# Layer one of a Fourier mix and two expert layers: ScalarE's relus ahead of its side work, stage A behind four result products

## Chip, cores and metric

The kernel runs on one core of one Trainium2 chip. Its five engines work through queues of their own, in order: TensorE (PE, with the weight loads as PEld), VectorE (DVE), ScalarE (ACT), GpSimd (POOL) and SyncE (SP, which issues most DMAs). The metric is the device time of one execution in microseconds. In the tables a result of TensorE lies in PSUM, in banks of 512 columns of float32; everything else lies in SBUF.

## What is computed

```python
X = fft(fft(x, axis=1), axis=2).real          # x: 2 x 3008 x 256
h = X @ w_in                                  # 6016 tokens, 256 -> 2048
g = maximum(h, 0) + alpha * minimum(h, 0)
x2 = g @ w_out                                # 2048 -> 256
h2 = x2 @ w_in2
out = (h2 * sigmoid(h2)) @ w_out2             # 256 -> 2048 -> 256
```

All matrices are float32, and products are made from parts: a value is split in a high part and the rest ("hi" and "lo"), and three products (hi hi, lo hi, hi lo) stand for one.

## The kernel before

The sequence transform is done as a transform of 47 by 64 points. For batch 0 it is done at the start (stage U, then psB). For batch 1 a stage A (`back_stage_a`) runs beside layer one: a piece of x is loaded (`xr`), split into `xhl` by ScalarE (line 367) and GpSimd (line 371), multiplied by a constant (`stage_a`, lines 377 to 379, tile psA), copied out by ScalarE as `ev` (line 406) and written to DRAM (`tmid`). There are 16 such pieces. Stage B (`stage_b`, psB, line 422) makes the tokens' features `pq` from it, again as hi (line 437) and lo (line 441). `rank_one` (psR, line 482, copied out as `rsb` in line 485) makes a row that is added to the even products. The tiles psA, psB, psR and psW share one PSUM bank (tag "x").

Layer one is a loop over 6 chunks `c` of 512 tokens (450 in the first) and 16 blocks `m` of 128 hidden units, 96 steps. In a step TensorE makes the even and the odd half of h in one bank (`products1`, line 602, three matmuls each). `column1` (line 622, VectorE) reads the bank after the even products, as `h`. Line 645 (VectorE) gets the mirrored token's value from the bank and `h`, into the bank psd ("h2"). Lines 646 and 647 (ScalarE) are the relus of both, into `r`, and line 651 (VectorE, twice) finishes the activation in `r`; it reads the bank too, so the bank is free only after its first half. There are two banks "h", two tiles `r`, three `gh` and two `gl`.

`close1`, called at the start of the next step, copies `r` to `gh` (ScalarE, line 666) and takes the rest to `gl` (GpSimd, line 667). The result products (`second1`, line 682, 12 matmuls a step: eight with `gh`, then four with `gl`) are kept in a queue, and `pull(n)` issues n of them. With `LAG1` = 1, a step pulls the products of two steps earlier.

`step1` also issues the even products of the next step ahead (`ahead`), if they are ready. All other work is written as generators that stop at phases: `advance(AMID)` and the like run them on by one stop. EARLY lies at the start of a step, before `close1`. At BANK the lo copies of psB and psW (lines 441, 576) are issued. At AMID come stage A's products with `ev`, psR with `rsb`, and the conversions of weights from 64 bit (`narrow`: lines 227 and 228 on ScalarE), and differences of the halves. At MID1 and MID2 come the later parts of the conversions (lines 233, 235) and, in the first step of all, a column sum (psS, line 559) and the mix of weight block 2 (`early_mix`, psW, line 553).

So the queue of each engine follows the order in which `step1` calls these. Before, it is: odd products, even products of the next step, eight result products, BANK, AMID, four result products, psd, relus, `column1` of the next step, line 651, then MID1 to MID3.

Of the kernel before, what the change touches and what calls it, by code (L numbers as in the profile page):

```python
# [25 lines left out]
NF = DFF // P  # L26
KG = 4
CK = 8
NC = B * H1 // CK
# [13 lines left out]
def _width(c):  # L43

    return AT0 + OWN if c == 0 else CK * N2
# [52 lines left out]
def kernel(  # L98
# [54 lines left out]
    def ptile(shape, name, tag="x"):  # L153
        return psh.tile(shape, F32, name=name, tag=tag, bufs=2 if tag == "h" else 1)

    def wtile(shape, dtype, name, tag):
        return work.tile(shape, dtype, name=name, tag=tag, bufs=BUFS[tag])
# [10 lines left out]
    EARLY, AMID, LATE, BANK, MID1, MID2, MID3 = range(1, 8)  # L168
    active = []

    def advance(phase):
        for job in list(active):
            if job[1] == phase:
                job[1] = next(job[0], 0)
                if not job[1]:
                    active.remove(job)
# [420 lines left out]
    def products1(c, m, eo, bank):  # L597

        w = _width(c)
        q, mm = divmod(m, 4)  # L600
        for a, bb in ((0, 0), (1, 0), (0, 1)):
            T.matmul(bank[:, :w], wa[q][:, mm, eo, a, :], pq[c][:, 2 * eo + bb, :w], start=eo == 0 and a == bb,  # L602
                     stop=bb == 1, skip_group_check=True)

    def ready1(c, m):

        if c == 0:
            return m // 2 in mixed and m // 2 in sums
        return c in rows and (c != HOST or guests) and sum(k == c for k, _ in turned) == CK // KG

    def even(c, m):

        assert ready1(c, m)
        bank = ptile([P, 512], "psh", "h")
        products1(c, m, 0, bank)
        return bank

    def column1(c, m, bank):

        w = _width(c)  # L620
        t = wtile([P, 512], F32, "h", "h")
        V.scalar_tensor_tensor(t[:, :w], pb[c][:, :w], wst[:, m:m + 1], bank[:, :w], op0=ALU.mult, op1=ALU.add)  # L622
        evens[c, m] = bank, t

    def step1(c, m):

        w = _width(c)
        n = 12 if len(queue) > LAG1 else 0
        if (c, m) not in evens:
            column1(c, m, even(c, m))  # L630
            pull(min(n, 8))
            n -= min(n, 8)
        bank, t = evens.pop((c, m))
        assert c in rows
        products1(c, m, 1, bank)
        c1, m1 = divmod(c * NF + m + 1, NF)
        ahead = even(c1, m1) if c1 < NC and ready1(c1, m1) else None
        pull(min(n, 8))
        n -= min(n, 8)
        advance(BANK)  # L640
        advance(AMID)
        pull(n)
        r = wtile([P, 2, 512], F32, "r", "r")
        other = ptile([P, 512], "psd", "h2")
        V.scalar_tensor_tensor(other[:, :w], t[:, :w], 2.0, bank[:, :w], op0=ALU.mult, op1=ALU.subtract)  # L645
        A.activation(r[:, 0, :w], bank[:, :w], AF.Relu, scale=-1.0)  # L646
        A.activation(r[:, 1, :w], other[:, :w], AF.Relu, scale=-1.0)
        if ahead is not None:
            column1(c1, m1, ahead)
        for s, h in enumerate((bank, other)):  # L650
            V.scalar_tensor_tensor(r[:, s, :w], r[:, s, :w], al[:, m:m + 1], h[:, :w], op0=ALU.mult, op1=ALU.add)  # L651
        save_due()
        advance(MID1)
        advance(MID2)
        advance(MID3)
        return c, m, r
# [34 lines left out]
    def save_due():  # L691
        while due:
            save_x2(due.pop())
# [20 lines left out]
    def pull(n):  # L714

        while n and queue:
            if next(queue[0], 0) is None:
                n -= 1
            else:
                queue.pop(0)  # L720
# [232 lines left out]
    with tc.manual_schedule():  # L953
# [30 lines left out]
        for i in range(nx):  # L984
# [5 lines left out]
            if i in BEHIND:  # L990
                kind, n = BEHIND[i]
# [59 lines left out]
        for eo, h in ((0, 0), (0, 1), (1, 0), (1, 1)):  # L1051
            n = CK // 2
# [61 lines left out]
        for c in range(NC):  # L1114
            for m in range(NF):
                early(c * NF + m)
                close1(last)
                last = step1(c, m)
                advance(LATE)
# [93 lines left out]
```

## Time and profile before

| | us |
|---|---|
| median of 3 runs | 966.06 (964.96 to 966.13) |
| the profiled execution | 965.77 |
| its span, first to last instruction | 964.0 |
| TensorE matmuls busy | 946.1 (98%) |
| TensorE weight loads busy | 792.3 (82%) |
| VectorE / ScalarE / GpSimd busy | 630.2 / 588.3 / 529.6 |

The profile is of one execution. A matmul is shown from its start to a modelled end, so that matmuls in sequence overlap. "Idle before" of a row is the time that its engine stood before it, with the instruction that released it. Layer one's steps lie between some 29 and 476 us.

### The profile page before, as it was taken

What the parts mean: (1) busy time and instruction counts of PE and PEld (TensorE: products, weight loads), DVE (VectorE), ACT (ScalarE), POOL (GpSimd) and SP (SyncE); (2) the same over time, 40 slices, a digit from 0 to 9 for tenths busy, and PEclk for the clock granted to TensorE, in tenths of its full rate; (3) what the DMA queues carried; (4) which work ended last, traced back from release to release, by engine and by line L of the source; (5) the groups of instructions that cost most, each with busy time, mean ns of one, the idle gap of its engine ahead of it and who ended that gap; (6) DMA issues with size and microseconds to landing.
All of it is one profiled execution on the core that took longest, in us unless ns stands there. A gap on an engine that the chain in (4) does not pass through costs nothing.

```text
span 964.0 us, 12344 instructions
## 1 busy us (share of the span) xinstructions
PE 946.1 (98%) x4351; PEld 792.3 (82%) x4351; DVE 630.2 (65%) x953; ACT 588.3 (61%) x996; POOL 529.6 (55%) x347
## 2 busy tenths in 40 slices
PE   9899999998999999999999999999999999999998
PEld 9799876776888878888899988888888888888886
DVE  4667654675777678777576765676576566657554
ACT  5787655565666557656666664665575565556654
POOL 0488767564456458998985733543354254334322
PEclk9999999999999999999999999999999999999999
DMA  9411112213422320021010020010010001001001
GB/s 330 151 44 50 33 50 69 71 48 111 161 66 99 110 66 23 1 66 33 12 44 23 1 83 1 1 44 1 1 44 1 1 1 44 1 1 45 0 1 45
DMA packets 30394, 47.60 MB, mean 49 GB/s; under 512 B 4118, under 2 KB 11388, under 8 KB 30076
## 3 DMA queue, kind: packets, MB, share of 16 engines
q1 hardware_dynamic: 29756, 45.98, 14.9%
q8 instruction: 34, 0.56, 0.2%
q10 hardware_dynamic: 576, 0.84, 0.2%
q14 instruction: 28, 0.23, 0.1%
HBM read 33.28 MB, written 13.52 MB: 49 GB/s over the span
## 4 chain that ended last, share of the span: by engine, by line
PE 94%; ACT 2%; DVE 2%; issue 1%; POOL 0%; ACTq 0%; POOLq 0%; DVEq 0%
PE pso L878 27%; PE pso L682 24%; PE psh L808 23%; PE psh L602 13%; PE psB L422 2%; PE psU L1015 2%; DVE r L651 1%; PE psW L553 1%; ACT r L646 1%; PE psA L379 0%; ACT raw L228 0%; PE psA L377 0%; PE psA L378 0%; PE idle L966 0%; PE psB L1055 0%
## 5 line engine op out<-in xcount | busy, mean ns | idle before, releaser
L829 DVE TENSOR_TENSOR ring<-ring,psh 128x512 f32<-128x512 f32 (+1 forms) x336 | 222.3, 674 | 168.3 <-PE psh L808 156.1
L878 PE MATMUL pso<-ghl,wAo 128*128 128x512 f32 (+1 forms) x1152 | 309.8, 385 | 0.0
L667 POOL TENSOR_TENSOR gl<-r,gh 128x1024 fp32r<-128x1024 f32 (+1 forms) x96 | 226.6, 2361 | 103.2 <-ACT gh L666 84.5
L808 PE MATMUL psh<-ts,wi 128*128 128x512 f32 (+1 forms) x1008 | 278.9, 385 | 0.0
L820 POOL TENSOR_TENSOR ghl<-ring,ghl 128x512 fp32r<-128x512 f32 (+1 forms) x96 | 137.6, 1433 | 255.5 <-ACT ghl L815 175.7
L878 PEld LDWEIGHTS pso<-ghl,wAo 128*128 128x128 f32 x1152 | 216.3, 188 | 40.6
L832 ACT ACTIVATE ring<-ring 128x512 f32<-128x512 f32 (+1 forms) x192 | 119.7, 623 | 178.0 <-DVE ring L829 176.1
L808 PEld LDWEIGHTS psh<-ts,wi 128*128 128x128 f32 x1008 | 189.3, 188 | 35.3
L682 PE MATMUL pso<-gh,wo_o 128*128 128x512 f32 (+1 forms) x768 | 187.8, 386 | 0.0
L682 PEld LDWEIGHTS pso<-gh,wo_o 128*128 128x128 f32 x768 | 144.3, 188 | 27.6
L602 PE MATMUL psh<-pq,wa 128*128 128x512 f32 (+1 forms) x576 | 153.7, 395 | 12.6 <-DVE r L651 10.2
L602 PEld LDWEIGHTS psh<-pq,wa 128*128 128x128 f32 x576 | 105.1, 188 | 41.7 <-DVE r L651 19.7
L666 ACT ACTIVATE gh<-r 128x1024 fp32r<-128x1024 f32 (+1 forms) x96 | 100.2, 1043 | 63.1 <-DVE r L651 60.3
L651 DVE SCALAR_TENSOR_TENSOR r<-r,al,psh 128x512 f32<-128x512 f32 (+1 forms) x96 | 70.8, 737 | 80.4 <-ACT r L646 77.2
L815 ACT ACTIVATE ghl<-ring 128x512 fp32r<-128x512 f32 (+1 forms) x192 | 119.2, 621 | 6.1
L682 PE MATMUL pso<-gl,wo_o 128*128 128x512 f32 (+1 forms) x384 | 102.2, 387 | 0.0
L645 DVE SCALAR_TENSOR_TENSOR psd<-h,psh 128x512 f32<-128x512 f32 (+1 forms) x96 | 65.5, 682 | 43.1 <-PE psh L602 41.0
L682 PEld LDWEIGHTS pso<-gl,wo_o 128*128 128x128 f32 x384 | 71.8, 188 | 13.9
L820 DVE TENSOR_TENSOR ghl<-ring,ghl 128x512 fp32r<-128x512 f32 (+1 forms) x96 | 76.6, 798 | 5.5 <-ACT ghl L815 5.3
L646 ACT ACTIVATE r<-psh 128x512 f32<-128x512 f32 (+1 forms) x96 | 55.8, 581 | 31.9 <-DVE psd L645 30.0
L622 DVE SCALAR_TENSOR_TENSOR h<-pb,wst,psh 128x512 f32<-128x512 f32 (+1 forms) x96 | 70.4, 734 | 1.6 <-PE psh L602 1.5
L651 DVE SCALAR_TENSOR_TENSOR r<-r,al,psd 128x512 f32<-128x512 f32 (+1 forms) x96 | 70.2, 732 | 0.0
(97 smaller groups left out, 647.3 us busy)
## 6 DMA issues: line engine op xcount, KB each, us to landing
raw<-in_w_in SPq DMA_DIRECT2D x16, 512.0 KB, 5.7
raw<-in_w_out SPq DMA_DIRECT2D x16, 512.0 KB, 5.0
out_dram<-ob SPq DMA_DIRECT2D x19, 256.0 KB, 2.3
x<-in_x SPq DMA_DIRECT2D x6, 512.0 KB, 6.0
xr<-in_x SPq DMA_DIRECT2D x16, 192.0 KB, 2.6
tmid<-ev SPq DMA_DIRECT2D x48, 64.0 KB, 1.7
ur<-tmid SPq DMA_DIRECT2D x6, 512.0 KB, 7.2
stash_o<-y SPq DMA_DIRECT2D x8, 256.0 KB, 3.2
```

The costliest lines, as they stand in the source:

```text
L602: T.matmul(bank[:, :w], wa[q][:, mm, eo, a, :], pq[c][:, 2 * eo + bb, :w], start=eo == 0 and a == bb, stop=bb == 1, skip_group_check=True)
L622: V.scalar_tensor_tensor(t[:, :w], pb[c][:, :w], wst[:, m:m + 1], bank[:, :w], op0=ALU.mult, op1=ALU.add)
L651: V.scalar_tensor_tensor(r[:, s, :w], r[:, s, :w], al[:, m:m + 1], h[:, :w], op0=ALU.mult, op1=ALU.add)
L666: A.activation(hi[:, :, :w], r[:, :, :w], AF.Copy)
L667: G.tensor_tensor(lo[:, :, :w], r[:, :, :w], f32(hi[:, :, :w]), op=ALU.subtract)
L682: T.matmul(po[c][s][k][:, :w], wo1[q][:, mm, a, k * P:(k + 1) * P], g[:, s, :w], start=m == 0 and a == 0 and g is hi, stop=m == NF - 1 and ...
L808: T.matmul(bank[j][:, :w], wi2[p][:, FORMS[j], a], t[:, :w], start=a == 0 and t is hi, stop=t is lo)
L815: A.activation(outs[p, i][:, 0, :w], g[:, :w], AF.Copy)
L820: eng.tensor_tensor(hl[:, 1, :w], g[:, :w], f32(hl[:, 0, :w]), op=ALU.subtract)
L829: V.tensor_tensor(dst[:, :w], a[:, :w], bank[j][:, :w], op=ALU.add)
L832: A.activation(a[:, :w], a[:, :w], AF.Silu)
L878: T.matmul(po[c, 2][s][k][:, :w], wo2[q][:, mm + m, a, k * P:(k + 1) * P], outs[p, i][:, g, :w], start=p == 0 and i < 2 and a == 0 and g == 0,
```

## The change

In `step1` the relus (and line 645) are now issued before `advance(BANK)` and `advance(AMID)`, so the side work of a step comes behind them on ScalarE, and the lo copies behind line 645 on VectorE. `column1` of the next step comes behind BANK but ahead of the result products. These are pulled as four, then AMID, then eight, where it was eight, BANK, AMID, four. Where a step's even products are not issued yet (the first step of a chunk whose inputs were not ready), and nothing can be pulled (the very first step), the even products of the next step and `advance(MID1)` come ahead of the odd products.

```diff
--- before.py
+++ after.py
@@ -626,27 +626,32 @@
 
         w = _width(c)
         n = 12 if len(queue) > LAG1 else 0
+        following = divmod(c * NF + m + 1, NF)
+        ahead = None
         if (c, m) not in evens:
             column1(c, m, even(c, m))
-            pull(min(n, 8))
-            n -= min(n, 8)
+            if n:
+                pull(8)
+                n -= 8
+            else:
+                ahead = even(*following)
+                advance(MID1)
         bank, t = evens.pop((c, m))
         assert c in rows
         products1(c, m, 1, bank)
-        c1, m1 = divmod(c * NF + m + 1, NF)
-        ahead = even(c1, m1) if c1 < NC and ready1(c1, m1) else None
-        pull(min(n, 8))
-        n -= min(n, 8)
-        advance(BANK)
-        advance(AMID)
-        pull(n)
+        if ahead is None and following[0] < NC and ready1(*following):
+            ahead = even(*following)
         r = wtile([P, 2, 512], F32, "r", "r")
         other = ptile([P, 512], "psd", "h2")
         V.scalar_tensor_tensor(other[:, :w], t[:, :w], 2.0, bank[:, :w], op0=ALU.mult, op1=ALU.subtract)
         A.activation(r[:, 0, :w], bank[:, :w], AF.Relu, scale=-1.0)
         A.activation(r[:, 1, :w], other[:, :w], AF.Relu, scale=-1.0)
+        advance(BANK)
         if ahead is not None:
-            column1(c1, m1, ahead)
+            column1(*following, ahead)
+        pull(min(n, 4))
+        advance(AMID)
+        pull(n - min(n, 4))
         for s, h in enumerate((bank, other)):
             V.scalar_tensor_tensor(r[:, s, :w], r[:, s, :w], al[:, m:m + 1], h[:, :w], op0=ALU.mult, op1=ALU.add)
         save_due()
```

Lines behind the change are numbered five higher in the changed kernel: 645, 646, 647, 651, 666, 667 and 682 become 646, 647, 648, 656, 671, 672 and 687.

ScalarE in a stage A step with a conversion, before (`gh` of the step before, then `ev`, the conversion, the relus):

```order
L666 ACTIVATE gh<-r 128x1024
L406 ACTIVATE ev<-psA 96x512
L227 ACTIVATE y_1856<-raw_1817 128x512
L228 ACTIVATE raw_1817<-raw_1817 128x512
L646 ACTIVATE r<-psh 128x512
L647 ACTIVATE r<-psd 128x512
L666 ACTIVATE gh<-r 128x1024
```

and in the changed kernel:

```order
L671 ACTIVATE gh<-r 128x1024
L647 ACTIVATE r<-psh 128x512
L648 ACTIVATE r<-psd 128x512
L406 ACTIVATE ev<-psA 96x512
L227 ACTIVATE y_1856<-raw_1817 128x512
L228 ACTIVATE raw_1817<-raw_1817 128x512
L671 ACTIVATE gh<-r 128x1024
```

`ev` and the two conversions moved behind the two relus.

TensorE around a stage A product, before (psh are the even and odd products, pso the result products):

```order
L602 MATMUL psh<-pq_927,wa_232 128x512 x6
L682 MATMUL pso<-gh,wo_o_355 128x512 x8
L377 MATMUL psA<-xhl,cat 96x512
L378 MATMUL psA<-xhl,cat 96x512
L379 MATMUL psA<-xhl,cat 96x512
L682 MATMUL pso<-gl,wo_o_355 128x512 x4
L602 MATMUL psh<-pq_927,wa_232 128x512 x3
L602 MATMUL psh<-pq_927,wa_388 128x512 x3
```

and in the changed kernel:

```order
L602 MATMUL psh<-pq_927,wa_232 128x512 x6
L687 MATMUL pso<-gh,wo_o_355 128x512 x4
L377 MATMUL psA<-xhl,cat 96x512
L378 MATMUL psA<-xhl,cat 96x512
L379 MATMUL psA<-xhl,cat 96x512
L687 MATMUL pso<-gh,wo_o_355 128x512 x4
L687 MATMUL pso<-gl,wo_o_355 128x512 x4
L602 MATMUL psh<-pq_927,wa_232 128x512 x3
L602 MATMUL psh<-pq_927,wa_374 128x512 x3
```

The three psA matmuls moved from behind the eighth to behind the fourth result product.

TensorE at the start of layer one, before (the last psB of the start, then psh: even 0, odd 0, even 1):

```order
L1055 MATMUL psB<-cbt,u_all 128x64 x8
L602 MATMUL psh<-pq_117,wa_232 128x450 x9
L559 MATMUL psS<-ones,wq 128x2 x2
L553 MATMUL psW<-wq,cwt 128x256 x4
L602 MATMUL psh<-pq_117,wa_232 128x450 x6
L422 MATMUL psB<-cbt,u_all 128x64 x8
L602 MATMUL psh<-pq_117,wa_232 128x450 x6
```

and in the changed kernel:

```order
L1060 MATMUL psB<-cbt,u_all 128x64 x8
L602 MATMUL psh<-pq_117,wa_232 128x450 x6
L559 MATMUL psS<-ones,wq 128x2 x2
L553 MATMUL psW<-wq,cwt 128x256 x4
L602 MATMUL psh<-pq_117,wa_232 128x450 x9
L422 MATMUL psB<-cbt,u_all 128x64 x8
L602 MATMUL psh<-pq_117,wa_232 128x450 x6
```

Odd 0 moved behind psS and psW: ahead of these now stand even 0 and even 1, behind them odd 0, odd 1 and even 2.

VectorE in the same first steps, before (h is `column1`):

```order
L622 SCALAR_TENSOR_TENSOR h<-pb,wst,psh 128x450
L645 SCALAR_TENSOR_TENSOR psd<-h,psh 128x450
L622 SCALAR_TENSOR_TENSOR h<-pb,wst,psh 128x450
L651 SCALAR_TENSOR_TENSOR r<-r,al,psh 128x450
L651 SCALAR_TENSOR_TENSOR r<-r,al,psd 128x450
L233 TENSOR_SCALAR y_359<-y_359 128x512
L576 TENSOR_TENSOR wa_388<-psW,wa_388 128x2x2x128
L645 SCALAR_TENSOR_TENSOR psd<-h,psh 128x450
```

and in the changed kernel:

```order
L622 SCALAR_TENSOR_TENSOR h<-pb,wst,psh 128x450
L646 SCALAR_TENSOR_TENSOR psd<-h,psh 128x450
L576 TENSOR_TENSOR wa_374<-psW,wa_374 128x2x2x128
L622 SCALAR_TENSOR_TENSOR h<-pb,wst,psh 128x450
L656 SCALAR_TENSOR_TENSOR r<-r,al,psh 128x450
L656 SCALAR_TENSOR_TENSOR r<-r,al,psd 128x450
L233 TENSOR_SCALAR y_359<-y_359 128x512
L646 SCALAR_TENSOR_TENSOR psd<-h,psh 128x450
```

The lo copy of psW (line 576) moved ahead of the second `column1`.

## Rows read from the trace of the kernel before

**Rows 1.** The page, parts 1 and 5: totals, and three groups of layer one

```profile
PE 946.1 (98%) x4351; PEld 792.3 (82%) x4351; DVE 630.2 (65%) x953; ACT 588.3 (61%) x996; POOL 529.6 (55%) x347
...
L667 POOL TENSOR_TENSOR gl<-r,gh 128x1024 fp32r<-128x1024 f32 (+1 forms) x96 | 226.6, 2361 | 103.2 <-ACT gh L666 84.5
...
L651 DVE SCALAR_TENSOR_TENSOR r<-r,al,psh 128x512 f32<-128x512 f32 (+1 forms) x96 | 70.8, 737 | 80.4 <-ACT r L646 77.2
...
L645 DVE SCALAR_TENSOR_TENSOR psd<-h,psh 128x512 f32<-128x512 f32 (+1 forms) x96 | 65.5, 682 | 43.1 <-PE psh L602 41.0
```

**Rows 2.** Busy us of each engine by stretch, then clock, DMA share, GB/s

```profile
30.00:42.00 12.00, 9.27 (x45) 7.89 (x44) 7.60 (x13) 7.08 (x17) 4.90 (x4) 0.86 0.21 70
33.80:37.00 3.20, 3.20 (x11) 2.71 (x10) 2.49 (x5) 1.05 (x3) 0.32 (x1) 0.50 0.00 0
42.00:105.00 63.00, 62.92 (x320) 57.49 (x320) 44.29 (x73) 47.49 (x87) 53.67 (x34) 1.00 0.14 44
105.00:244.00 139.00, 129.78 (x563) 101.11 (x561) 81.55 (x119) 80.22 (x129) 86.18 (x44) 1.00 0.27 73
360.00:480.00 120.00, 120.00 (x532) 99.59 (x531) 87.45 (x124) 78.84 (x119) 109.02 (x76) 1.00 0.10 30
```

**Rows 3.** Waits of TensorE's matmuls: us, times, longest

```profile
PE psh L602 <- DVE r L651: 10.2, 17, 1.5
```

**Rows 4.** Waits of TensorE's weight loads: us, times, longest

```profile
PEld psh L602 <- DVE r L651: 19.7, 25, 1.9
```

**Rows 5.** Timeline, TensorE, two plain steps: start, us, engine, line, tile

```profile
292.13 1.98 PE L682 MATMUL pso<-gh,wo_o 128*128 128x512 f32 x8
...
296.21 1.98 PE L682 MATMUL pso<-gh,wo_o 128*128 128x512 f32 x8
```

**Rows 6.** Timeline of a step with stage A

```profile
155.73 0.40 PE L377 MATMUL psA<-xhl,cat 96*96 96x512 f32 x1
...
156.43 1.09 PE L682 MATMUL pso<-gl,wo_o 128*128 128x512 f32 x4
156.67 0.60 ACT L406 ACTIVATE ev<-psA 96x512 f32<-96x512 f32 x1 [1.86 <-PE psA L379]
...
157.17 0.59 ACT L646 ACTIVATE r<-psh 128x512 f32<-128x512 f32 x1
...
157.35 0.84 PE L602 MATMUL psh<-pq,wa 128*128 128x512 f32 x3
...
158.59 0.98 PE L602 MATMUL psh<-pq,wa 128*128 128x512 f32 x3 [0.40 <-DVE r L651]
...
161.26 0.39 PE L377 MATMUL psA<-xhl,cat 96*96 96x512 f32 x1
```

**Rows 7.** Stage A's first products, all: durations, first and last start

```profile
L377 PE MATMUL psA<-xhl,cat x16: 392/396/397, 105.0 to 231.9; 96*96 96x512 f32 x16
```

**Rows 8.** Timeline of a stage A step with a conversion

```profile
202.46 0.65 ACT L227 ACTIVATE y<-raw 128x512 f32<-128x512 f32 x1
...
202.69 0.84 PE L602 MATMUL psh<-pq,wa 128*128 128x512 f32 x3
...
204.97 0.97 PE L602 MATMUL psh<-pq,wa 128*128 128x512 f32 x3 [1.44 <-DVE r L651]
```

**Rows 9.** Timeline, a conversion without stage A

```profile
352.02 0.98 PE L602 MATMUL psh<-pq,wa 128*128 128x512 f32 x3 [0.99 <-DVE r L651]
```

**Rows 10.** Timeline of layer one's first two steps

```profile
31.76 0.66 DVE L622 SCALAR_TENSOR_TENSOR h<-pb,wst,psh 128x450 f32<-128x450 f32 x1
...
32.57 1.65 PE L602 MATMUL psh<-pq,wa 128*128 128x450 f32 x6 [2.27 <-DVE h L622]
...
34.73 3.12 PE L553 MATMUL psW<-wq,cwt 128*128 128x256 f32 x8
...
37.50 1.58 PE L602 MATMUL psh<-pq,wa 128*128 128x450 f32 x6
...
42.65 0.57 PE L682 MATMUL pso<-gh,wo_o 128*128 128x450 f32 x2
```

## Prediction

> **What bounds the kernel now.** I read the totals by engine first, then the busy time by stretch, then who waits for whom, and the order of time last. The totals show a kernel bound by TensorE: 946.1 of 964.0 us, the other engines at two thirds or less [rows 1]. So a gain can only come from time in which TensorE does not issue. The stretches say where that is [rows 2]: 30 to 42 us (9.27 of 12 busy, with the granted clock at its lower level, 0.50, for 3.2 us) and 105 to 244 us (129.78 of 139). From 42 to 105 and from 360 to 480 next to nothing is lost. The waits name the cause: 17 times TensorE stood before line 602 until VectorE's line 651 had run, 10.2 us in all [rows 3]. The same wait seen from the weight loads is 19.7 us in 25 times [rows 4]. The first figure is too small, since a matmul is drawn until its result is out, long after the next could have been issued; the second is too large, since a weight load normally runs ahead. The loss lies between.
>
> The order of time shows the chain. `even` of step m+2 needs the bank of step m, which line 651 releases, and that follows the relu of line 646 on ScalarE. In a step with a stage A product [rows 6], `ev` (line 406) stands ahead of the relu, and ScalarE waits 1.86 us for psA, the last side work of TensorE there. Only then come the relu (157.17) and line 651, and TensorE, which began its odd products at 157.35, is held before the next even ones until 158.59. psA to psA takes 161.26 - 155.73 = 5.53 us in this step. A step without side work takes 296.21 - 292.13 = 4.08 us [rows 5] for 18 products (0.227 us each), and the three psA products 156.43 - 155.73 = 0.70 us: 4.78 us in all. So **0.7 us is lost in a psA step**. There are 16 psA from 105.0 to 231.9 [rows 7]. In three of their steps the two conversions of a weight block (lines 227 and 228, 0.65 us each) stand between `ev` and the relu as well, and three odd products (0.68 us) then take 204.97 - 202.69 = 2.28 us [rows 8]: 1.6 us are lost, and with the drain behind it 1.7. A conversion without psA holds TensorE for 0.99 us more at 352 us [rows 9].
>
> **The change, part by part.** No instruction is added or removed. The queues of SP and GpSimd keep their order, so nothing is moved past a DMA there.
>
> *Relus first (removes waits).* On ScalarE the relus now follow `gh` of the step before, and `ev`, `rsb` and the conversions come behind them. Let a step's odd products end at 0. VectorE's psd (line 645, 0.68) ends near 0.9; the relu (0.59) starts after it, as it does in the trace, and ends at 1.5; VectorE's line 622, of the same kind and shape as 651, runs beside it until 1.65, and 651 (0.74) ends near 2.4 [rows 1, 6]. The bank is wanted after the next even products, twelve result products, psA and the next odd ones, at 4.78 in a psA step and 4.08 in a plain one. So 1.7 us or more is spare and the wait goes. Saved: 13 x 0.7 = 9.1, 3 x 1.7 = 5.1, 1.0 at 352 us, and some smaller holds behind psR and conversions that I take at 0.7. **Sum 15.9 us**, between 10.2 and 19.7 as it must be.
>
> *psA and psR behind four products instead of eight.* The products beside them are the same twelve. psA now ends near 2.4, after the second relu, so ScalarE takes `ev` at once and keeps up: it is busy 80.22 of 139 us [rows 2], and `gh` waits for nothing that is later than before. `gl` (2.36 us on GpSimd) is wanted only a step later still. What is late next: in a step with psB the lo copy of line 441 now stands behind psd (0.68), and a psA or psR four products later must wait for the shared bank. The bounds are 0 and 0.68 in each of some five steps, 0 to 3.4 us; I take 0.7 us in all, since six and four products (2.3 us) cover most of it.
>
> *The first step.* Before, TensorE stands 2.27 us until line 622, begun at 31.76, is done, and starts at 32.57 [rows 10]; then its clock is at 0.50 from 33.8 to 37.0 [rows 2], so that psW takes 37.50 - 34.73 = 2.77 us, about twice its time at the higher level. After, `even` of step one, psS and psW fill the gap (0.6 for three products of 450 columns, 0.2 and 1.4 us), and the odd products of step zero start at nearly the same 32.6. But VectorE then has psd, the lo copy of psW and 622 of step one in a row, 2 us at some 0.7 each after the odd products end at 33.3, so a new gap of 2 us opens before the second odd products, until 35.5. From there the work up to the first result product is the same as from 37.50 before, and that took 42.65 - 37.50 = 5.15 us: 40.6. **A gain of 2.0 us.** The upper end is 3.0, if the waits in those 5.15 us are not repeated; the lower end is 0.4, if the clock falls after the new gap as it did after the old one and half of 3.2 us is lost again. The stretch from 42 to 105 has TensorE without loss, so what is gained is carried on.
>
> *Sum.* 15.9 + 2.0 - 0.7 = 17.2 us. The profiled execution took 965.77 us around its span of 964.0, so it would be 948.6; the median of the three runs is 0.3 above it, and the forecast is **948.9 us**. TensorE is then busy nearly throughout, so the bound stays where it is.
>
> *A rule against it.* The hold repeats in psA step after psA step, 0.4 us of idle TensorE before line 602 [rows 6]; but with the same two banks there is none in the plain steps [rows 5]. That speaks for the time a bank is held, not for the number of banks. The Trainium skill, Perfetto Trace Analysis, section Optimization Strategy, says that consistent bubbles can mean that SBUF or PSUM lack room for the next tile; by that reading another order on the same two banks would give nothing here, and it is the second rival below.
>
> **The rivals.**
>
> *Another release takes the place of line 651.* The relu also writes `r`, of which there are two, so it needs `gl` of two steps earlier on GpSimd. For it speaks that steps shrink from 5.5 to 4.8 us while GpSimd's `gl` of 2.36 and the `xhl` difference stay. Against it, GpSimd is busy only 86.18 of 139 us there [rows 2]. If half of the 15.9 us came back, the time would be 966.1 - 8.0 - 2.0 + 0.7 = 956.8 us.
>
> *The bubble is one of bank number.* Then only the first step gains: 966.1 - 2.0 = 964.1 us, or no change at all where the clock takes that back too. Plain steps without a gap speak against it.
>
> *Slower: the side work becomes late.* Conversions now wait for two relus of 0.59, some 1.2 us, and GpSimd's differences wait for the conversions. From 42 to 105 GpSimd is busy 53.67 of 63 us, from 360 to 480 109.02 of 120 [rows 2]: 9.3 + 11.0 = 20.3 us are spare. Those stretches hold 63 / 4.7 + 120 / 4.08 = 42 steps (4.7 for a step with some side work). If every one lost the whole 1.2 us, GpSimd would be 50 - 20 = 30 us short, TensorE would wait for `gl` before its last four result products, and the time would be 948.9 + 30 = 979 us. It makes the kernel slower only if GpSimd loses more than 20.3 + 17.2 = 37.5 us, in three steps of four. Against it: in plain steps nothing stands behind the relus, and `gh` with its `gl` comes ahead of them in either order.
>
> *The order is not what it says.* The instruction lists show that relus and psA did move, so this gets no chance of its own.
>
> **How the numbers follow.** Forecast 0.77; half comes back 0.14; bank number 0.05 (of it 0.02 with no gain in the first step either); slower 0.04. Around the forecast itself the ends of the first step (0.4 to 3.0), of the psB wait (0 to 3.4) and of the holds (up to 19.7) give 944.8 to 953; to leave no more than two in ten outside I take in the first rival, up to 956.8. About 0.2%, 1.9 us, is what a measurement of this kernel can tell from no change. The bank-number case at 964.1 just clears it, so: faster 0.93, same 0.03, slower 0.04.
>
> **What would show it.** Right: line 602's wait for line 651 falls below 1.5 us on TensorE; psA to psA is 4.8 us; the relu stands ahead of `ev` and does not wait for it; 105 to 244 us becomes a stretch without loss; the first result product starts between 39.6 and 42.2. Wrong: TensorE waits for 651 while ScalarE's relu waits for GpSimd's `gl` (first rival); the gap before line 602 stays in psA steps though the relu is early (second); TensorE waits for `gl` at line 682's place in 42 to 105 or 360 to 480 (third).

## The result, and the profile after

The changed kernel took **949.41 us** (median of 5 runs, 947.29 to 950.22) against 965.72 us (5 runs, 964.96 to 966.13): a ratio of 0.9827, with a 95% interval of 0.981 to 0.9843, so 16.3 us or 1.7% faster. The profiled execution took 950.22 us around a span of 948.4.

The page, part 1 (busy us, share of the span, instructions), of the changed kernel, against [rows 1]:

```profile
PE 940.7 (99%) x4351; PEld 795.5 (84%) x4351; DVE 632.6 (67%) x953; ACT 589.3 (62%) x996; POOL 529.8 (56%) x347
```

The same instructions ran for much the same time on the engines beside TensorE; TensorE's own 946.1 us fell to 940.7. A matmul before a hold is drawn to its modelled end (three odd products take 0.84 us in [rows 6], six products 1.52 us below), so a part of the holds had counted as busy time: line 602's products of 512 columns alone fell from 129.3 to 123.4 us. What went is time in which TensorE did not issue. The busy time by stretch shows where, against [rows 2] (layer one is shorter now, so the later stretches lie earlier):

```profile
33.80:35.85 2.05, 0.14 (x1) 0.00 (x0) 1.87 (x4) 1.63 (x5) 0.00 (x0) 1.00 0.00 1
36.90:43.50 6.60, 6.60 (x27) 6.24 (x26) 4.19 (x9) 4.62 (x9) 5.68 (x4) 0.50 0.24 83
42.00:105.00 63.00, 63.00 (x318) 57.73 (x317) 45.75 (x73) 47.23 (x88) 52.99 (x34) 0.99 0.11 36
105.00:229.00 124.00, 124.00 (x558) 101.80 (x557) 83.67 (x121) 80.26 (x128) 86.22 (x44) 1.00 0.30 78
345.00:465.00 120.00, 120.00 (x533) 99.56 (x532) 86.15 (x123) 78.55 (x119) 108.87 (x75) 1.00 0.09 27
```

From 105 to 229 us TensorE is busy without a gap, where 9.2 of 139 us were missing. GpSimd's 86.22 us now lie in 124 us. The first two rows are the other half of the story: a gap of 2 us in the first steps, and after it 6.6 us at the lower clock.

The waits of TensorE's matmuls before line 602, then those of its weight loads for line 656 and the one of ScalarE's relu for `gl` on GpSimd (us, times, longest), against [rows 3, 4]:

```profile
PE psh L602 <- DVE h L622: 2.4, 2, 1.9
```

```profile
PEld psh L602 <- DVE r L656: 0.2, 1, 0.2
```

```profile
ACT r L647 <- POOL gl L672: 1.2, 1, 1.2
```

Of 17 waits for line 651 (now 656) on the matmuls none is left, of 25 on the weight loads one of 0.2 us. A psA step in order of time, against [rows 6]:

```profile
150.69 0.60 ACT L647 ACTIVATE r<-psh 128x512 f32<-128x512 f32 x1 [1.24 <-DVE psd L646]
...
151.28 0.40 PE L377 MATMUL psA<-xhl,cat 96*96 96x512 f32 x1
...
151.32 0.75 DVE L656 SCALAR_TENSOR_TENSOR r<-r,al,psh 128x512 f32<-128x512 f32 x1
...
152.18 0.60 ACT L406 ACTIVATE ev<-psA 96x512 f32<-96x512 f32 x1 [0.40 <-PE psA L379]
...
153.81 1.52 PE L602 MATMUL psh<-pq,wa 128*128 128x512 f32 x6
...
156.08 0.40 PE L377 MATMUL psA<-xhl,cat 96*96 96x512 f32 x1
```

The relu runs 1.5 us ahead of `ev`, line 656 is done at 152.07, and the six even and odd products at 153.81 come in one piece. ScalarE waits 0.40 us for psA instead of 1.86. psA to psA is 156.08 - 151.28 = 4.80 us, where it was 5.53. All 16 psA, as the view of line 377 gives them, against [rows 7]:

```profile
L377 PE MATMUL psA<-xhl,cat x16: 396/396/443, 104.6 to 218.9; 96*96 96x512 f32 x16
```

They span 114.3 us, where it was 126.9: 12.6 of the gain lie here. TensorE in the first steps, of the kernel before (even 0, the line ahead of those in [rows 10]) and of the changed one (even 0 and even 1):

```profile
29.45 0.85 PE L602 MATMUL psh<-pq,wa 128*128 128x450 f32 x3
```

```profile
29.66 1.49 PE L602 MATMUL psh<-pq,wa 128*128 128x450 f32 x6
...
31.35 1.97 PE L553 MATMUL psW<-wq,cwt 128*128 128x256 f32 x8
32.97 0.97 PE L602 MATMUL psh<-pq,wa 128*128 128x450 f32 x3
35.85 1.70 PE L602 MATMUL psh<-pq,wa 128*128 128x450 f32 x6 [1.91 <-DVE h L622]
37.35 3.51 PE L422 MATMUL psB<-cbt,u_all 128*128 128x64 f32 x16
...
43.01 2.16 PE L687 MATMUL pso<-gh,wo_o 128*128 128x450 f32 x8
```

The old gap is filled and the new one is there, before the odd products of step one, at 35.85. But the first result product starts at 43.01, not earlier than the 42.65 of before: psB, 16 matmuls, takes 3.3 us to the next products at the lower clock. From even 0 to the first result product it is 42.65 - 29.45 = 13.20 us before and 43.01 - 29.66 = 13.35 us now. So in this execution the whole gain lies behind the first result product: 964.0 - 42.65 = 921.35 us before, 948.4 - 43.01 = 905.4 now, **16.0 us less**.

### The profile page after: what moved, and what is told of

It is laid out like the page before. It is cut to its first block, busy times and chain, and to the rows that moved or that the text cites. A ratio compares the mean times of both kernels' runs of the same rounds, so it can differ in the third digit from the quotient of the medians.

```text
span 948.4 us, 12361 instructions
## 1 busy us (share of the span) xinstructions
PE 940.7 (99%) x4351; PEld 795.5 (84%) x4351; DVE 632.6 (67%) x953; ACT 589.3 (62%) x996; POOL 529.8 (56%) x347
## 3 DMA queue, kind: packets, MB, share of 16 engines
q1 hardware_dynamic: 29756, 45.98, 15.2%
## 4 chain that ended last, share of the span: by engine, by line
PE 99%; DVE 0%; DMA 0%; ACT 0%; issue 0%
PE pso L687 27%; PE pso L883 27%; PE psh L813 24%; PE psh L602 14%; PE psB L422 2%; PE psU L1020 2%; PE psW L553 1%; PE psA L377 0%; PE psA L379 0%; PE psA L378 0%; DMA const<-in_a 0%; PE psB L1060 0%; DVE psd L646 0%; DVE h L622 0%; PE psR L482 0%; PE psP L1072 0%
## 5 line engine op out<-in xcount | busy, mean ns | idle before, releaser
L687 PE MATMUL pso<-gh,wo_o 128*128 128x512 f32 (+1 forms) x768 | 191.8, 387 | 0.0
L602 PE MATMUL psh<-pq,wa 128*128 128x512 f32 (+1 forms) x576 | 148.7, 393 | 2.4 <-DVE h L622 2.4
L602 PEld LDWEIGHTS psh<-pq,wa 128*128 128x128 f32 x576 | 107.9, 190 | 23.3 <-DVE h L622 3.5
```

The costliest lines, as they stand in the source:

```text
L687: T.matmul(po[c][s][k][:, :w], wo1[q][:, mm, a, k * P:(k + 1) * P], g[:, s, :w], start=m == 0 and a == 0 and g is hi, stop=m == NF - 1 and ...
```

## The experiments

All were timed over five rounds, each beside the kernel before on the same chip. My theory: a bank was held because its relu stood behind side work on ScalarE, and relus first is enough. Rival A: the earlier place of psA does it. Rival B: the first step does it.

**Relus only.** The relus and psd go ahead, the result products stay eight and four, the first step is the old one:

```diff
-        pull(min(n, 8))
-        n -= min(n, 8)
-        advance(BANK)
-        advance(AMID)
-        pull(n)
         r = wtile([P, 2, 512], F32, "r", "r")
...
         A.activation(r[:, 1, :w], other[:, :w], AF.Relu, scale=-1.0)
+        pull(min(n, 8))
+        n -= min(n, 8)
+        advance(BANK)
+        advance(AMID)
+        pull(n)
```

> Only the relus (and psd) move ahead of side work; psA stays behind eight result products, the first step is the old one. Theory (a bank is held because its relu stands behind the side work on ScalarE, so relus first is enough): all of the 15.9 us go, 965.7 - 15.9 = 949.8 us, and TensorE waits for line 651 (its number in this kernel may differ) below 1 us. Rival A (the earlier place of psA does it): no gain or at most a third, 960 us or more. Rival B (the gain comes from the first step): 965.7.

Measured: 949.37 us, ratio 0.9829 (0.9816 to 0.9843). The wait is gone from TensorE's matmuls, and on the weight loads this is left:

```profile
PEld psh L602 <- DVE r L651: 0.2, 1, 0.2
```

The relus alone do all that the change does in the median. Rival B falls, and rival A is not needed; whether it would do by itself is the next run's question.

**Four only.** The side work goes behind four result products, the relus stay behind it:

```diff
-        pull(min(n, 8))
-        n -= min(n, 8)
+        pull(min(n, 4))
+        n -= min(n, 4)
```

> Only the side work's place among the result products changes, four instead of eight ahead of it; the relus stay behind it, the first step is the old one. Theory: psA ends 0.9 us earlier, so ev, relu and 651 do too; the hold of 0.7 us in 13 psA steps just goes (9.1), and the three with a conversion lose 0.8 instead of 1.7 us (2.7 saved), the one at 352 us stays: 965.7 - 11.8 = 953.9 us. Rival A: all of it, 949.8. Rival B: 965.7.

Measured: 951.9 us, ratio 0.9854 (0.9839 to 0.9869). Matmuls, then weight loads:

```profile
PE psh L602 <- DVE r L651: 1.6, 3, 0.6
```

```profile
PEld psh L602 <- DVE r L651: 4.2, 7, 1.0
```

So each half of the change takes away most of the holds by itself, and they don't add: psA 0.9 us earlier is already enough for a plain psA step (4.79 us from psA to psA), and three holds are left, of at most 0.6 us, each behind a psA step with a conversion. It saved 2 us more than I had reckoned (13.9 against 11.8): I had let the conversion at 352 us and the small holds stand whole, though the side work of those steps moved too; on the matmuls none of them is left. Rival A is thus nearly a cure of its own, by the same release: psA earlier lets `ev`, the relu and line 651 run earlier.

**The first step only.**

```diff
+            if n:
+                pull(8)
+                n -= 8
+            else:
+                ahead = even(*divmod(c * NF + m + 1, NF))
+                advance(MID1)
```

> Only the first step of all has the new order (even 0, even 1, psS and psW ahead of odd 0). Theory: between 963.2 and 966.1 us, because the clock at the start decides: where it falls after the new gap the first result product starts no earlier than before (43.0 against 42.65 in the profiles), where it does not some 2.5 us are gained. TensorE's waits for line 651 stay near 10.2 us. Rival B: 950.

Measured: 966.69 us (11 runs, 963.95 to 967.31), ratio 1.0004 (0.9995 to 1.0013): no gain, and the median lies 0.6 us above the range that I had given. The wait for line 651 (here 657) is whole, and the granted clock of 36 to 43 us is at its lower level nearly throughout (0.52 is the mean, after the busy times):

```profile
PE psh L602 <- DVE r L657: 10.2, 17, 1.5
```

```profile
36.00:43.00 7.00, 7.00 (x28) 6.60 (x28) 4.49 (x9) 4.94 (x9) 5.45 (x4) 0.52 0.26 76
```

**The old first step in the changed kernel.** The branch of the last diff is taken out.

> The changed kernel with the old first step (odd 0 ahead of even 1, psS and psW). Theory: 965.7 - 15.9 = 949.8 us, with a smaller spread than the changed kernel's 947.3 to 950.2, since the old first step always has the same low clock. Rival B: 963 or more.

Measured: 950.1 us (948.81 to 950.32), ratio 0.9835 (0.9821 to 0.9848). Together with the run before this puts the new first step at 0.9 us lost by itself and 0.7 gained with the relus first, both within what the runs tell apart: nothing in the median. The spread is smaller, as expected (1.5 us against 2.9).

**The gap filled.** To see whether the clock takes the first step's gain, TensorE gets nine more products into a bank that nobody reads, while it waits:

```diff
         products1(c, m, 1, bank)
+        if (c, m) == (0, 0):
+            junk = pso.tile([P, 512], F32, name="junk", tag="o")
+            for _ in range(9):
+                T.matmul(junk[:, :w], wa[0][:, 0, 0, 0, :], pq[0][:, 0, :w], start=True, stop=True)
```

> The changed kernel with nine extra products of 450 columns behind odd 0, into a bank that nobody reads: TensorE works through the 2 us in which it waits for line 622 of step one. Theory (the first step gained nothing in the median because the clock falls after that gap; runs at 947.3 are those where it does not): the granted clock stays at its upper level from 24 to 42 us, the first result product starts near 40.7, all runs are at 947.3 us or up to 0.3 above. Rival: the clock is set by something else, or the gap costs nothing: 949.4 us or more, spread as before.

Measured: **946.36 us** (946.13 to 947.21), ratio 0.9801 (0.9788 to 0.9815). Busy time by stretch, then TensorE in order of time:

```profile
30.00:42.00 12.00, 11.92 (x68) 10.71 (x67) 10.00 (x18) 9.98 (x21) 6.75 (x5) 1.00 0.28 88
```

```profile
28.75 1.47 PE L602 MATMUL psh<-pq,wa 128*128 128x450 f32 x6
...
32.85 1.99 PE L645 MATMUL junk<-pq,wa 128*128 128x450 f32 x9
34.92 1.49 PE L602 MATMUL psh<-pq,wa 128*128 128x450 f32 x6
36.25 1.89 PE L422 MATMUL psB<-cbt,u_all 128*128 128x64 f32 x16
37.95 1.49 PE L602 MATMUL psh<-pq,wa 128*128 128x450 f32 x6
39.27 1.81 PE L691 MATMUL pso<-gh,wo_o 128*128 128x450 f32 x8
```

The clock stays at 1.00, and the first result product starts at 39.27. Every one of its runs is below every run of the changed kernel, by more than I had expected (947.3 us, and 40.7 for the first result product); 0.9 us of the 39.27 is only that even 0 starts earlier in this execution. The nine products do no useful work and don't shorten the gap: from even 0 to the odd products of step one it is 34.92 - 28.75 = 6.17 us, and 6.19 in the changed kernel. Behind the gap it is 39.27 - 34.92 = 4.35 us to the first result product, against 43.01 - 35.85 = 7.16: 2.8 us less, of which psB alone has 1.6 (1.70 us to the next products against 3.27). That shows that the clock after the gap is what ate the first step's gain. It fits that the runs of the changed kernel itself have two levels: the two whose mean granted clock was 0.998 and 1.0 took 947.29 and 947.37 us, the three at 0.996 took 949.41 to 950.22. The mean clock does not order all runs, though: with the first step only, the eight runs at 0.996 took 965.81 to 967.31 us and two at 0.998 and 1.0 took 964.1 and 963.95, but a third, at 1.0, took 966.96. Something besides the clock moves single runs by some 2 us: in the profiled executions of all the kernels even 0 starts between 28.49 and 30.73 us, though the work ahead of it is the same.

**Column1 first.** `column1` of the next step goes ahead of `advance(BANK)`, so that the gap in the first step is shorter:

```diff
-        advance(BANK)
         if ahead is not None:
             column1(*following, ahead)
+        advance(BANK)
```

> The changed kernel with column1 (line 622) ahead of the lo copies of psB and psW on VectorE, in all steps. Theory: the first gap is 0.7 us shorter (1.2 instead of 1.9), so 948.7 us in the median, or about 946.8 where the clock stays up; in later steps the lo copy comes 0.7 us later and psA or psR behind psB may wait up to 0.7 us in five steps, so at most 3.4 us are given back. Rival: the lo copy was not what line 622 stood behind: 949.4.

Measured: 951.18 us (947.94 to 952.55), ratio 0.9843 (0.9825 to 0.9862). Of TensorE's waits, the first is the gap; the other three are new, each for a lo copy that stands behind 622 now and holds the bank of psA, psR and psW:

```profile
PE psh L602 <- DVE h L622: 1.3, 1, 1.3
...
PE psW L553 <- DVE wa L576: 0.7, 1, 0.7
PE psR L482 <- DVE pq L441: 0.6, 1, 0.6
PE psA L377 <- DVE pq L441: 0.6, 1, 0.6
```

The gap shrank to 1.3 us, but the clock fell all the same in the profiled run (its mean is 0.996), and the 1.9 us of these waits, with two of 0.3 us for line 656 that are new as well, outweigh the 0.6. I had expected 946.8 to 948.7, with up to 3.4 us given back. With six products to fill the shorter gap as well:

> Column1 ahead of the lo copies and six extra products in the gap that is then left. Theory: no low clock and the first result product near 40.0: 946.6 us, the fastest so far, in all runs alike. Rival: as in the two alone, 948.7 or more.

Measured: 948.4 us (947.98 to 950.29), ratio 0.9825 (0.9811 to 0.9838): 2.0 us behind the filled gap alone and 1.8 above what I had expected: the same three waits are in its profile. In the profiled execution, 950.29 us, the clock did not fall in layer one; there even 0 starts at 30.73, 2 us later than with the filled gap alone.

**Release late.** The halves of line 656 are swapped, to see how much time is spare before the bank is wanted:

```diff
-        for s, h in enumerate((bank, other)):
+        for s, h in ((1, other), (0, bank)):
```

> The changed kernel with the two halves of line 656 (651 before) swapped, so that each bank is released 0.74 us later. Theory (1.7 us are spare after the change, 1.0 would be left in a plain step): no change, 949.4 us within 1 us, and TensorE does not wait for this line. Rival (the two banks are still what TensorE runs into): 0.1 to 0.74 us in each of up to 96 steps, 955 us or more.

Measured: 953.48 us (952.86 to 954.06), ratio 0.9873 (0.986 to 0.9887): 4 us slower than the change, so my expectation failed (3.5 us beside the three runs of the change with the same mean clock, 0.996). Weight loads, then the largest case in order of time:

```profile
PEld psh L602 <- DVE r L656: 4.9, 10, 1.4
```

```profile
257.18 1.09 PE L687 MATMUL pso<-gl,wo_o 128*128 128x512 f32 x4
...
258.18 0.96 PE L602 MATMUL psh<-pq,wa 128*128 128x512 f32 x3
...
260.13 0.96 PE L602 MATMUL psh<-pq,wa 128*128 128x512 f32 x3 [0.98 <-DVE r L656]
```

In most steps the later release costs nothing, so two banks are not what TensorE runs into there. But ten steps wait. In the one shown, behind the first step of a chunk, eight result products had been issued ahead of that step's odd products, so that only four stand between these and the next pair; the spare time that I had worked out for twelve does not exist. The wait of 0.90 us at 334.60 has the same order, and the one of 0.68 us at 36.05 lies in the first steps of all, which have no result products yet. The other seven are of 0.17 to 0.36 us, on the weight loads alone; in six of them VectorE had side work of the step before (lines 233, 235 or 705) ahead of line 646, which makes the chain to the release longer than I had reckoned.

**Back to eight, and the lo copies first, both with the gap filled.** With the clock quiet at the start, small terms can be priced. The first puts psA and psR behind eight result products again; the second puts the lo copies of psB and psW back ahead of psd in all steps but the first:

```diff
-        pull(min(n, 4))
+        pull(min(n, 8))
         advance(AMID)
-        pull(n - min(n, 4))
+        pull(n - min(n, 8))
```

> The kernel with the filled gap (e5_fill, 946.36 us), with psA and psR back behind eight result products. With the clock quiet at the start, this prices the place of psA more finely than the first runs. Theory (with the relus first the place is worth next to nothing): 946.4 us within 0.5. Rival A (psA's earlier place has a gain of its own): 947 us or more.

```diff
+        if (c, m) != (0, 0):
+            advance(BANK)
         V.scalar_tensor_tensor(other[:, :w], t[:, :w], 2.0, bank[:, :w], op0=ALU.mult, op1=ALU.subtract)
...
-        advance(BANK)
+        if (c, m) == (0, 0):
+            advance(BANK)
```

> The kernel with the filled gap (e5_fill), with the lo copies of psB and psW ahead of psd on VectorE again, as before the change, in all steps but the first. Theory (the lo copy behind psd costs next to nothing, since the products ahead of psA and psR cover it): 946.4 us within 0.5. Rival (it costs what I put down for it): 945.7 us.

Measured: 946.81 us (945.83 to 947.63), ratio 0.9802 (0.9789 to 0.9815), and **945.31 us** (945.15 to 946.87), ratio 0.979 (0.9777 to 0.9804). The place of psA is worth nothing that these runs can tell once the relus are first. The lo copies ahead of psd give the lowest median of all, 1.0 us below the filled gap, as the rival had it and not the theory; since the intervals of the two overlap, the sign of this last step is likely but not settled. The changed kernel shows one place where the lo copy costs time, at the start of a chunk: `column1` stands behind it on VectorE, and TensorE's even and odd products wait for `column1`.

```profile
330.33 0.68 DVE L441 TENSOR_TENSOR pq<-psB,pq 128x512 fp32r<-128x512 f32 x1
...
330.94 0.74 DVE L622 SCALAR_TENSOR_TENSOR h<-pb,wst,psh 128x512 f32<-128x512 f32 x1
...
331.73 1.67 PE L602 MATMUL psh<-pq,wa 128*128 128x512 f32 x6 [0.45 <-DVE h L622]
```

With the lo copies ahead of psd, the waits of TensorE's matmuls list none for line 622. Both kernels beat the changed one, by 2.6 and 4.1 us.

## Why the prediction was right, point by point

- *The holds, 15.9 us.* Right in cause and size. The part behind the first result product is 16.0 us shorter, with 15.2 in the sum (15.9 less the 0.7 for the lo copies). Term by term, from psA to psA: the thirteen intervals without a conversion became 9.05 us shorter together (9.1 in the sum), two with a conversion 1.75 and 1.78 us (1.7 each), and behind the last psA 2.6 us went (2.7, for the third conversion and the one at 352 us). The run with the relus alone shows the cause. That two banks are enough once they are released in time is shown by the same two banks now giving no hold on the matmuls. The Trainium skill (Perfetto Trace Analysis, Optimization Strategy) says that such a repeating gap can mean too little room; more room was not needed here. Whether a third bank would have taken the holds away in the old order no run shows.
- *psA behind four products.* The sum had nothing for it but the cost of 0.7 us for the lo copies. Alone it takes away 13.9 us, beside the relus nothing, so the change has two cures for one illness. The 0.7 us are of the size that the last run points to, but not where the prediction had them: no psA or psR waits for its bank in the changed kernel, and the one wait behind a lo copy, beside the gap in the first steps, is that of line 602 for `column1` at 331.73, 0.45 us.
- *The first step, 2.0 us.* This term failed: in the profiled execution it gave -0.4 us, below its lower end of 0.4 (0.2 of that lies ahead of even 0, which starts at 29.66 instead of 29.45). The sign that hung on it failed too: the first result product starts at 43.01 and not between 39.6 and 42.2. The gap came where and as long as I had put it (1.91 us, from the odd products to 35.85). The step that failed is the price of the clock: I had taken it as a lower end of 0.4 us, by the 3.2 us at the lower clock of before, and put the likeliest value at a clock that stays up. It fell for 6.6 us in the profiled run, twice as long as I had taken, and two more runs of the five have the same mean clock, 0.996. With the clock up the term is larger than 2.0: even 0 to the first result product takes 39.27 - 28.75 = 10.52 us with the gap filled, against 13.20 in the kernel before, so 2.7 us. A small slip beside it: psW, put at 1.4 us for the higher clock, takes 32.97 - 31.35 = 1.62, so the 2.77 us before, nearly all at the lower clock, were 1.7 times that and not twice.
- *The sum, 948.9 us,* missed the median by 0.5 us, and that is in part luck. In the profiled execution, from which the terms are read, the span fell by 15.6 us where the sum has 17.2: the first step gave 2.4 us less than its term, and the rest 0.8 more (the stretch from the first result product to the first psA is 104.6 - 43.01 = 61.6 us, before 105.0 - 42.65 = 62.4). The median of the five lies 0.8 us below this execution. The lower end of the range, 944.8, is not what its three terms give together: 948.9 - 1.0 - 0.7 - 3.8 = 943.4. Nothing hangs on that.
- *Rivals.* `gl` as the next release shows once, 1.2 us, and no TensorE wait follows from it. The rival of the bank number fell with the result. GpSimd is as busy from 345 to 465 as before (108.87 us of 120), and TensorE does not wait for `gl` there: the side work did not become late.
- *What was too broad.* "1.7 us or more is spare" does not hold in every step: it was worked out for twelve result products between two pairs, and the run with the late release found ten places with less.

## What to carry to other kernels

Where a buffer of a full engine is released through an in-order queue, look at what stands ahead of the releasing instruction there: side work that itself waits for that engine closes a loop, and moving the release ahead of it gave 16 us here, at the price of 0.45 us of waiting behind a lo copy. Two cures for one wait do not add, so try each alone before both are kept. And a gap can cost more than its length: the clock fell after one of 1.9 us here and took another 2.8 us, and filling the gap with products for nothing gave 3 us.

## What was not expected of the hardware

The granted clock fell in all eight profiled runs that have an unfilled TensorE gap of 1.3 to 2.3 us in the first steps. How long it stayed at its lower level went with the order of the first step and not with the length of the gap: 3.2 us or a little more in the four runs with the old first step (gaps of 2.25 to 2.28 us), 6.6 us or a little more in the four with the new one (1.31 to 2.18 us). Why, no run shows. Nor is the fall certain: of the five runs of the changed kernel one has a mean clock of 1.0, and one has 0.998, which the kernel before has with its 3.2 us. So a gap of this length has no fixed price here. The two levels of the changed kernel, 2 us or more apart, go with the mean clock, but part of what separates single runs is the start of even 0, which moves by up to 2.2 us between profiled executions.
